# Moving a routing exponential from the first to the second half of a tile's routing

## The chip, the cores and the metric

The kernel runs on one core of a Trainium2 chip. The metric is the device time of one execution in microseconds. Five engines share the work, each with its own queue that it takes in order: PE (TensorE, matmuls), DVE (VectorE), ACT (ScalarE), POOL (GpSimd) and SP (SyncE, which here only issues transfers).

## The reference, cut to what matters

Three layers follow each other. Block attention over 8 heads gives a token matrix x of 4608 rows and 512 columns. A dense layer maps it through 2048 hidden columns. A routed layer then sends each token to one of 8 experts:

```
out = softmax(q_c @ k_c.T / 8) @ v_c              # 64-row chunks
x   = relu(x @ w_in)**2 @ w_out                   # 512 -> 2048 -> 512
logits = x @ w_gate + modality_bias[modality_id]
e_idx  = argmax(logits);  probs = exp(logits - max)
gate   = probs[e_idx] / (sum(probs) + 1e-9)       # probs[e_idx] is exp(0) = 1
out[mask] = gate * (relu(x[mask] @ w1[e]) @ w2[e])
```

The changed instruction computes `exp(logits - max)` of one tile of 128 tokens, and with it the sum over the 8 experts. Only that sum is used: the gate is one over it.

## The kernel before, in words

The 4608 tokens are 36 tiles of 128. Nine blocks of four tiles pass through the dense layer one after the other. For a block, `mm1` runs 16 steps of 12 matmuls (x times w_in, in three 16-bit passes), and `mm2` runs 16 steps of 12 matmuls (hidden times w_out, four steps a tile). After the nine blocks comes the expert stage: `slot_mm1` and `slot_mm2` take 128 gathered rows of one expert at a time.

One mm1 step fills one PSUM tile `hp`, of which there are two. ACT must empty it with a Relu (`r<-hp`) before the step after the next can start. From `r`, ACT makes a 16-bit square (`big<-r`), DVE a 32-bit square (`g<-r`), and POOL their difference. Five tiles `r` exist.

Attention of later tiles, the splitting of the expert weights (`piece_split`: ACT writes `wss`, DVE its low half, SP stores it; one buffer) and the routing of finished tiles run beside this on ACT, DVE, POOL and SP, with a few small matmuls on PE.

Routing of tile i begins when its last mm2 step is done: `x2_evac` (ACT and DVE take the result out of PSUM into `xs`), `x2_tr` (SP transposes it), then two halves. `route_a` has 12 small matmuls into `lp`, seven DVE instructions (`lg`, the maximum, its index in two instructions, `ef`, `oh`, `nm`) and, before the change, the Exp on ACT (`ex<-lg,nm`, which also sums into `se`). `route_b` has two small matmuls into `rp`, DVE's `dj`, `di`, `run`, `ga`, its reciprocal and `mt`, and a POOL scatter of `mt` to DRAM (`meta`). `ga` is the first reader of `se`.

The order on every engine's queue is made once, when the program is written. Work beside the matmuls stands in a list with due times. Between two steps, `flush` issues what is due. An event whose engine is over its budget (`COST` gives each event a cost on ACT and on DVE, `back` sums it up) is put off, at most by 30 units of planned time; `route_a`, `route_b` and one small norm share a PSUM tile, and are kept two steps apart from each other. Then `evac` issues the Relu and what follows it for the step that was issued before, and then the next step's matmuls are issued. So the first event issued in a `flush` stands ahead of the Relu of the previous step on ACT's queue.

Of the kernel before, what the change touches and what calls it, by code (L numbers as in the profile page):

```python
# [8 lines left out]
F32 = mybir.dt.float32  # L9
# [4 lines left out]
AF = mybir.ActivationFunctionType  # L14
ALU = mybir.AluOpType
# [14 lines left out]
def kernel(  # L30
# [17 lines left out]
    E, _, F2 = w1.shape  # L48
# [18 lines left out]
    sm_p = ctx.enter_context(tc.tile_pool(name="sm", bufs=4))  # L67
# [17 lines left out]
    def act(out, in_, func=AF.Copy, **kw):  # L85
        nc.scalar.activation(out=out, in_=in_, func=func, **kw)  # L86

    def stt(out, in0, s, in1, op0, op1, **kw):
        nc.vector.scalar_tensor_tensor(out=out, in0=in0, scalar=s, in1=in1, op0=op0, op1=op1, **kw)  # L89

    def ts2(out, in0, s1, s2, op0, op1=None, eng=None):
        if op1 is None:
            (eng or nc.vector).tensor_scalar(out=out, in0=in0, scalar1=s1, scalar2=None, op0=op0)  # L93
        else:
            (eng or nc.vector).tensor_scalar(out=out, in0=in0, scalar1=s1, scalar2=s2, op0=op0, op1=op1)  # L95
# [486 lines left out]
    def route_a(i):  # L582
        a = x2[i]
        lp = ps_r.tile([128, 512], F32, tag="r", name="lp")
        n = 0
        for la, lb in PASSES:
            for kk in range(KD):
                nc.tensor.matmul(lp[:, 0:E], lhsT=a["xt"][:, la * KD + kk, :], rhs=wgs[:, lb, kk, :],
                                 start=n == 0, stop=n == 3 * KD - 1)
                n += 1  # L590
        lg = sm_p.tile([128, E], F32, tag="lg", name="lg")
        stt(lg, lp[:, 0:E], a["ui"][:, 0:1], bias_t[:, i, :], ALU.mult, ALU.add)
        m8 = sm_p.tile([128, 8], F32, tag="m8", name="m8")
        i8 = sm_p.tile([128, 8], U32, tag="i8", name="i8")
        nc.vector.max(out=m8, in_=lg)
        nc.vector.max_index(out=i8, in_max=m8, in_values=lg)
        ef = sm_p.tile([128, 1], F32, tag="ef", name="ef")
        nc.vector.tensor_copy(out=ef, in_=i8[:, 0:1])
        oh = sm_p.tile([128, E], F16, tag="oh", name="oh")
        ts2(oh, iota8, ef[:, 0:1], None, ALU.is_equal)  # L600
        nm = sm_p.tile([128, 1], F32, tag="nm", name="nm")
        ts2(nm, m8[:, 0:1], -1.0, None, ALU.mult)
        ex = sm_p.tile([128, E], F32, tag="ex", name="ex")
        se = sm_p.tile([128, 1], F32, tag="se", name="se")
        act(ex, lg, AF.Exp, bias=nm[:, 0:1], accum_out=se)
        a["oh"], a["se"] = oh, se

    def route_b(i):
        a = x2[i]
        rp = ps_r.tile([128, 512], F32, tag="r", name="rp")  # L610
        nc.tensor.matmul(rp[:, 0:E], lhsT=ones_h, rhs=run, start=True, stop=False)
        nc.tensor.matmul(rp[:, 0:E], lhsT=tri_h, rhs=a["oh"], start=False, stop=True)
        dj = sm_p.tile([128, E], F32, tag="dj", name="dj")
        df = sm_p.tile([128, 1], F32, tag="df", name="df")
        di = sm_p.tile([128, 1], I32, tag="di", name="di")
        stt(dj, rp[:, 0:E], 1.0, a["oh"], ALU.mult, ALU.mult, accum_out=df)
        nc.vector.tensor_copy(out=di, in_=df)
        nc.vector.tensor_tensor(out=run, in0=run, in1=a["oh"], op=ALU.add)
        mt = sm_p.tile([128, 2], F32, tag="mt", name="mt")
        nc.gpsimd.tensor_copy(out=mt[:, 0:1], in_=tok[:, i:i + 1])  # L620
        ga = sm_p.tile([128, 1], F32, tag="ga", name="ga")
        ts2(ga, a["se"], 1e-9, None, ALU.add)
        nc.vector.reciprocal(out=ga, in_=ga)
        ts2(mt[:, 1:2], ga, a["ui"][:, 0:1], SWG / (SW1 * SW2), ALU.mult, ALU.mult)
        nc.gpsimd.indirect_dma_start(  # L625
            out=meta[:, :], out_offset=bass.IndirectOffsetOnAxis(ap=di[:, 0:1].bitcast(U32), axis=0),
            in_=mt, in_offset=None,
        )
        x2.pop(i)
# [42 lines left out]
    def map_a1():  # L672
        assert (route_b, SEEN - 1) in done and (route_b, SEEN) not in done
        ci = counts(0.0, "a")
        tf = sm_p.tile([128, E], F32, tag="tf", name="tf")
        m8 = sm_p.tile([128, 8], F32, tag="m8", name="m8a")
        i8 = sm_p.tile([128, 8], U32, tag="i8", name="i8a")
        ea = const.tile([128, 1], F32, name="ea")
        on = const.tile([128, E], F32, name="on")
        rw = sm_p.tile([128, 1], F32, tag="rw", name="rwa")  # L680
        nc.vector.tensor_copy(out=tf, in_=ci)
        nc.vector.max(out=m8, in_=tf)
        nc.vector.max_index(out=i8, in_max=m8, in_values=tf)
        nc.vector.tensor_copy(out=ea, in_=i8[:, 0:1])
        ts2(rw, ea, float(TPE), None, ALU.mult)
        mp["mga"] = meta_gather(rw, EARLY, "a")
        ts2(on, iota8, ea[:, 0:1], None, ALU.is_equal)
        rg = const.tile([1, 1], I32, name="rga")
        nc.vector.tensor_copy(out=rg, in_=i8[0:1, 0:1])
        mp.update(ea=ea, on=on, rga=rg)  # L690
# [139 lines left out]
    def once(fn, s):  # L830
# [14 lines left out]
    COST = {  # L845
        attn_split: (0.95, 1.14), attn_vsplit: (1.04, 1.2), attn_max: (0.0, 1.2), attn_exp: (0.52, 0.0),
        attn_p: (0.0, 1.5), attn_psplit: (0.52, 0.0), attn_x: (0.48, 0.6), x_sq: (0.52, 0.0),
        x_norm: (0.0, 0.2), piece_split: (0.95, 1.14), x2_evac: (1.2, 1.1), route_a: (0.3, 0.9),
        route_b: (0.0, 0.8),
    }  # L850

    def uses_r(fn, a):
        return fn in (route_a, route_b) or fn is x_norm and where[a[0]][3] == 3
# [11 lines left out]
    def at_chain(chain):  # L865
# [3 lines left out]
        attn_split: ((attn_s, 2),), attn_s: ((attn_max, 1),), attn_max: ((attn_psplit, 2),),  # L869
        attn_psplit: ((attn_ptr, 2),), attn_vsplit: ((attn_pv, 2),), attn_ptr: ((attn_pv, 2),), attn_pt: ((attn_pv, 2),), attn_pv: ((attn_x, 1),),  # L870
        x_norm: tuple((x_sq, d) for d in range(4)), x2_evac: ((x2_tr, 4),), x2_tr: ((route_a, 2),), piece_split: ((piece_store, 1),),
        piece_load: ((piece_split, 4),),
    }
# [193 lines left out]
    for su, (b0, nt, sb) in enumerate(supers):  # L1067
        for j in sb:
            n = subs[j][1]
            ta = T  # L1070
            for c in range(KF * n // 4):
                steps.append((T, mm1, (j, c)))
                T += STEP
            span.append((ta, T))
        for t, qq in M2 if su == 0 else [(t, qq) for t in range(nt) for qq in range(4)]:
            steps.append((T, mm2, (su, t, qq)))
            T += STEP
            if qq < 3:
                continue
            i = b0 + t  # L1080
            d = (2.0, 7.0, 9.7) if i >= NTILE - 2 else (4.0, 11.0, 16.0)
            ch = [(T, x2_evac, (i,)), (T + d[0], x2_tr, (i,)), (T + d[1], route_a, (i,)), (T + d[2], route_b, (i,))]
            if i == SEEN - 1:
                ch += [(T + 20.0, map_a1, ()), (T + 30.0, map_a2, ()), (T + 35.0, once, (slot_gather, 0)),
                       (T + 35.1, once, (slot_gather, 1)), (T + 35.2, once, (slot_gather, 2)),
                       (T + 35.3, once, (slot_gather, 3)), (T + 45.0, once, (slot_tr, 0)),
                       (T + 50.0, once, (slot_tr, 1)), (T + 55.0, once, (slot_tr, 2)), (T + 60.0, once, (slot_tr, 3))]
            if i == NTILE - 1:
                ch += [(T + 12.4, map_b1, ()), (T + 18.4, map_b2, ()), (T + 18.5, once, (slot_w1, EARLY)),
                       (T + 18.6, once, (slot_w2, EARLY)), (T + 26.0, map_b3, ()),  # L1090
                       (T + 26.1, once, (slot_gather, EARLY)), (T + 26.2, once, (slot_gather, EARLY + 1)),
                       (T + 30.0, once, (slot_tr, EARLY)), (T + 32.0, once, (slot_tr, EARLY + 1))]
            at_chain(ch)
        if su == len(supers) - 1:
            for x, h, t in ((0, 0, 0.1 - STEP * 4 * nt), (0, 1, 0.2 - STEP * 4 * nt), (1, 0, 2.1), (1, 1, 20.0)):
                at_time(T + t, early_w, x, h)
# [154 lines left out]
```

## Time and profile before

| what | us |
|---|---|
| median of 3 runs | 1309.19 |
| lowest and highest | 1309.03, 1309.44 |
| the profiled execution's own time | 1314.08 |
| its span, first to last instruction | 1312.3 |

The profile describes one execution, which took 4.89 us longer than the median of the three runs. A timeline row gives the start of a group of equal instructions, its length and, in brackets, how long its engine sat idle before and what ended that. Ends of matmuls are modelled: the mean matmul of 512 columns lasts 380 ns, while in a group of 12 they start closer than that. The dense stage with attention and routing fills the span up to about 872 us, the expert stage the rest.

### The profile page before, as it was taken

The page shows a single profiled execution, that of the slowest core. Times are in us where ns is not written, and L with a number is a line of the kernel's source. Part 1 is how long each engine was busy: PE and PEld are TensorE (multiplying, and loading weights), DVE is VectorE, ACT ScalarE, POOL GpSimd, SP SyncE. Part 2 cuts the span into 40 slices and gives each one's busy share as a digit, 9 for nine tenths or more (in the row PEclk, how much of TensorE's full clock was granted, in tenths as well). Part 3 has the DMA queues.
Part 4 walks back from the last instruction along what each step waited for, and adds up shares of the span by engine and source line. Part 5 has one row for each costly group of instructions (what it writes and reads, how often), then busy time and mean ns, then how long its engine had stood idle before and what let it go on. Part 6 is the DMA issues. An engine that isn't in the chain of part 4 may idle for free.

```text
span 1312.3 us, 28854 instructions
## 1 busy us (share of the span) xinstructions
PE 1234.1 (94%) x11836; PEld 700.0 (53%) x11836; DVE 673.7 (51%) x1467; ACT 553.7 (42%) x978; POOL 407.3 (31%) x386
## 2 busy tenths in 40 slices
PE   5898999999999999999999999998999993999994
PEld 4444444445444444444444444466777772777773
DVE  6899785785876877867857836132111110111110
ACT  5887564563654654745645635211111110111110
POOL 4488351440431522422604604312122110111111
PEclk9899999999999999999999999999999996999998
DMA  9355536756477558477566451644223358322221
GB/s 376 140 186 147 113 113 190 197 170 200 133 222 174 159 154 227 124 201 179 167 195 162 139 135 33 201 83 157 69 77 82 79 168 186 74 73 74 74 73 41
DMA packets 172346, 188.54 MB, mean 144 GB/s; under 512 B 119547, under 2 KB 119587, under 8 KB 171186
## 3 DMA queue, kind: packets, MB, share of 16 engines
q1 hardware_dynamic: 128930, 157.72, 42.0%
q0 software_dynamic: 7376, 20.01, 4.8%
q10 hardware_dynamic: 35904, 8.92, 4.3%
q8 instruction: 94, 1.54, 0.5%
q14 instruction: 42, 0.34, 0.1%
HBM read 240.23 MB, written 53.08 MB: 224 GB/s over the span
## 4 chain that ended last, share of the span: by engine, by line
PE 43%; issue 22%; DMA 15%; DVE 12%; ACT 6%; POOL 0%; SPq 0%; POOLq 0%; DVEq 0%; ACTq 0%
PE op L558 23%; PE hp L543 14%; DMA out_dram<-o,tib 10%; DVE g L89 2%; DMA wsp<-wss 2%; PE xp L433 1%; DVE wss L89 1%; PE hp L805 1%; DMA big<-in_w_in_dram 1%; DVE qkt L89 1%; ACT r L86 1%; ACT wss L86 1%; ACT big L86 1%; DVE wl L89 1%; PE op L819 1%
## 5 line engine op out<-in xcount | busy, mean ns | idle before, releaser
L543 PE MATMUL hp<-xt,big 128*128 128x512 f16 x1728 | 387.7, 380 | 9.6 <-ACT r L86 9.4
L558 PE MATMUL op<-big,big 128*128 128x512 f16 x1728 | 384.5, 380 | 0.5 <-POOL big L523 0.5
L543 PEld LDWEIGHTS <-big 128*128 128x128 f16 x1728 | 164.1, 98 | 200.6 <-issue 14.7
L558 PEld LDWEIGHTS <-big 128*128 128x128 f16 x1728 | 165.1, 98 | 194.3 <-issue 2.8
L523 POOL TENSOR_TENSOR big<-g,big 128x512 f16<-128x512 f32 x144 | 177.1, 1234 | 209.3 <-DVE g L89 140.8
L89 DVE SCALAR_TENSOR_TENSOR ht<-hp,ht 128x512 f16<-128x512 f32 x74 | 51.2, 692 | 355.4 <-ACT ht L86 355.4
L805 PE MATMUL hp<-xgt,big 128*128 128x128 f16 x3552 | 210.0, 222 | 24.9 <-DMA xgt<-xg 24.9
L805 PEld LDWEIGHTS <-big 128*128 128x128 f16 x3552 | 206.3, 99 | 33.7 <-issue 25.6
L819 PE MATMUL op<-big,ht 128*128 128x512 f16 x888 | 197.6, 379 | 0.0
L89 DVE SCALAR_TENSOR_TENSOR g<-r,bq 128x512 f32<-128x512 f32 x138 | 136.9, 996 | 31.7 <-ACT r L86 30.6
L819 PEld LDWEIGHTS <-ht 128*128 128x128 f16 x888 | 85.4, 98 | 96.2
L825 POOL DMA_INDIRECT out_dram<-o,tib x33 | 33.5, 1014 | 291.4 <-ACT o L86 281.9
L89 DVE SCALAR_TENSOR_TENSOR wss<-wst,wss 128x1024 f16<-128x1024 f32 x64 | 91.5, 1430 | 60.5 <-ACT wss L86 59.9
L86 ACT ACTIVATE ht<-hp 128x512 f16<-128x512 f32 x74 | 44.2, 597 | 177.5 <-PE hp L805 177.4
L625 POOL DMA_INDIRECT meta<-mt,di x36 | 40.9, 1137 | 213.2 <-issue 81.1
L86 ACT ACTIVATE big<-r,bls 128x512 f16<-128x512 f32 x138 | 99.5, 722 | 6.5 <-DVE bli L95 0.7
L86 ACT ACTIVATE r<-hp 128x512 f32<-128x512 f32 x138 | 80.9, 587 | 48.2 <-PE hp L543 30.8
L86 ACT ACTIVATE wss<-wst 128x1024 f16<-128x1024 f32 x64 | 67.0, 1047 | 56.4 <-DMA wsp<-wss 37.5
L86 ACT ACTIVATE o<-op,fsb 128x512 f32<-128x512 f32 x33 | 22.7, 687 | 152.7 <-PE op L819 152.7
L406 POOL TENSOR_TENSOR ps<-ee,ps 128x512 f16<-128x512 f32 x32 | 44.2, 1381 | 89.8 <-ACT ps L86 88.4
L86 ACT ACTIVATE ex<-lg,nm 128x8 f32<-128x8 f32 x36 | 10.8, 301 | 116.4 <-DVE nm L93 116.4
L89 DVE SCALAR_TENSOR_TENSOR qkt<-qk,qkt 128x1024 f16<-128x1024 f32 x32 | 44.3, 1384 | 12.5 <-ACT qkt L86 11.7
(174 smaller groups left out, 984.2 us busy)
## 6 DMA issues: line engine op xcount, KB each, us to landing
big<-wsp SPq DMA_DIRECT2D x72, 2048.0 KB
wst<-in_w_dram SPq DMA_DIRECT2D x64, 512.0 KB
wsp<-wss SPq DMA_DIRECT2D x64, 512.0 KB
qk<-in_qk_dram SPq DMA_DIRECT2D x36, 512.0 KB
vv<-in_v_dram SPq DMA_DIRECT2D x36, 256.0 KB
x2d<-xs SPq DMA_DIRECT2D x36, 256.0 KB
big<-in_w_in_dram SPq DMA_DIRECT2D x16, 512.0 KB
wl<-in_w_out_dram SPq DMA_DIRECT2D x16, 512.0 KB
```

Of the source, the lines that this page charges most:

```text
L86: nc.scalar.activation(out=out, in_=in_, func=func, **kw)
L89: nc.vector.scalar_tensor_tensor(out=out, in0=in0, scalar=s, in1=in1, op0=op0, op1=op1, **kw)
L406: nc.gpsimd.tensor_tensor(out=a["ps"][:, 1], in0=pf, in1=a["ps"][:, 0], op=ALU.subtract)
L433: nc.tensor.matmul(xp[h, hp, 64 * c:64 * c + 64], lhsT=vs[h, la, c, hp, :], rhs=pt[h, lb * KD + hp, 64 * c:64 * c + 64], start=n == 0, sto ...
L523: nc.gpsimd.tensor_tensor(out=lo, in0=q32.rearrange("p (f n) -> p f n", f=nf), in1=hi, op=ALU.subtract)
L543: nc.tensor.matmul(hp[:, q_ * n:(q_ + 1) * n], lhsT=wi[:, la, kk, f * 128:f * 128 + 128], rhs=x[:, lb, kk, :], start=i == 0, stop=i == 3 * ...
L558: nc.tensor.matmul(ps, lhsT=g[:, la, f, t * 128:t * 128 + 128], rhs=wo[:, lb, f, :], start=f == 0 and n == 0, stop=f == KF - 1 and n == 2)
L625: nc.gpsimd.indirect_dma_start(out=meta[:, :], out_offset=bass.IndirectOffsetOnAxis(ap=di[:, 0:1].bitcast(U32), axis=0), in_=mt, in_offset ...
L805: nc.tensor.matmul(hp[:, f4 * 128:f4 * 128 + 128], lhsT=w[:, la, kk, f * 128:f * 128 + 128], rhs=xt[:, lb * KD + kk, :], start=n == 0, sto ...
L819: nc.tensor.matmul(ps, lhsT=ht[:, la, f, :], rhs=w[:, lb, f, :], start=f == 0 and n == 0, stop=f == KF2 - 1 and n == 2)
L825: nc.gpsimd.indirect_dma_start(out=out[:, :], out_offset=bass.IndirectOffsetOnAxis(ap=slot[s][0].bitcast(U32), axis=0), in_=o, in_offset=N ...
```

## The change

The three lines that allocate `ex` and `se` and issue the Exp leave `route_a` and stand in `route_b`, behind the update of `run`. `lg` and `nm` are kept for it. In the table `COST`, the 0.3 of ACT time moves from `route_a` to `route_b` too.

```diff
         nm = sm_p.tile([128, 1], F32, tag="nm", name="nm")
         ts2(nm, m8[:, 0:1], -1.0, None, ALU.mult)
-        ex = sm_p.tile([128, E], F32, tag="ex", name="ex")
-        se = sm_p.tile([128, 1], F32, tag="se", name="se")
-        act(ex, lg, AF.Exp, bias=nm[:, 0:1], accum_out=se)
-        a["oh"], a["se"] = oh, se
+        a["oh"], a["nm"], a["lg"] = oh, nm, lg
 
     def route_b(i):
...
         nc.vector.tensor_tensor(out=run, in0=run, in1=a["oh"], op=ALU.add)
+        ex = sm_p.tile([128, E], F32, tag="ex", name="ex")
+        se = sm_p.tile([128, 1], F32, tag="se", name="se")
+        act(ex, a["lg"], AF.Exp, bias=a["nm"][:, 0:1], accum_out=se)
         mt = sm_p.tile([128, 2], F32, tag="mt", name="mt")
         nc.gpsimd.tensor_copy(out=mt[:, 0:1], in_=tok[:, i:i + 1])
         ga = sm_p.tile([128, 1], F32, tag="ga", name="ga")
-        ts2(ga, a["se"], 1e-9, None, ALU.add)
+        ts2(ga, se, 1e-9, None, ALU.add)
...
-        x_norm: (0.0, 0.2), piece_split: (0.95, 1.14), x2_evac: (1.2, 1.1), route_a: (0.3, 0.9),
-        route_b: (0.0, 0.8),
+        x_norm: (0.0, 0.2), piece_split: (0.95, 1.14), x2_evac: (1.2, 1.1), route_a: (0.0, 0.9),
+        route_b: (0.3, 0.8),
```

Every engine issues the same instructions as before, in the same number; only their order differs. Up to planned step 39 of 288 the events fall into the same steps. From step 40 to step 249 attention, routing and weight pieces move by at most three steps either way, and from step 250 on each event is in its old step again.

On ACT, in the mm1 steps of the fourth block, where tile 14 is routed, before (r is the Relu's result, hp its PSUM tile; the numbers only tell buffers apart):

```order
L86 ACTIVATE r_6097<-hp 128x512
L86 ACTIVATE big_98<-r_6097,bls 128x512
L86 ACTIVATE ex,se<-lg,nm 128x8
L86 ACTIVATE r_6147<-hp 128x512
L86 ACTIVATE big_98<-r_6147,bls 128x512
L86 ACTIVATE xt<-xp 128x4x128
L86 ACTIVATE wss<-wst 128x1024
```

The same place on ACT now:

```order
L86 ACTIVATE r_6097<-hp 128x512
L86 ACTIVATE big_98<-r_6097,bls 128x512
L86 ACTIVATE r_6144<-hp 128x512
L86 ACTIVATE big_98<-r_6144,bls 128x512
L86 ACTIVATE xt<-xp 128x4x128
L86 ACTIVATE ps<-ee 128x512
L86 ACTIVATE wss<-wst 128x1024
```

The Relu that stood behind the Exp follows the square of the step before it directly; `ps`, which belongs to attention, comes a little earlier.

On ACT, six steps later, where the second half of tile 14's routing now stands:

```order
L86 ACTIVATE wss<-wst 128x1024
L86 ACTIVATE r_6318<-hp 128x512
L86 ACTIVATE big_98<-r_6318,bls 128x512
L86 ACTIVATE ex,se<-lg,nm 128x8
L86 ACTIVATE r_6358<-hp 128x512
L86 ACTIVATE big_98<-r_6358,bls 128x512
```

Here the Exp again stands ahead of a Relu, but its inputs `lg` and `nm` were made six steps earlier. Of the 36 Exps, 17 stood directly ahead of a Relu `r<-hp` before, and 23 do now.

On DVE, the second half of tile 14's routing now:

```order
L89 SCALAR_TENSOR_TENSOR wss<-wst,wss 128x1024
L89 SCALAR_TENSOR_TENSOR g_6320<-r_6318,bq 128x512
L89 SCALAR_TENSOR_TENSOR dj,df<-rp,oh 128x8
L614 CAST di<-df 128x1
L615 TENSOR_TENSOR run<-run,oh 128x8
L93 TENSOR_SCALAR ga<-se 128x1
L623 RECIPROCAL ga<-ga 128x1
L95 TENSOR_SCALAR mt<-ga,ui 128x1
L89 SCALAR_TENSOR_TENSOR g_6360<-r_6358,bq 128x512
```

DVE's instructions of this half and their order are the same as before; `ga` now reads a sum that ACT makes in the same half.

At the end of the routing, on ACT, from the Exps of tiles 33 and 34 to that of tile 35, the last (`xs` is taken out for tile 35; `ht` belongs to the expert stage), before:

```order
L86 ACTIVATE ex,se<-lg,nm 128x8 x2
L86 ACTIVATE xs,ss<-op 128x512
L86 ACTIVATE xs<-op,tss 128x512
L86 ACTIVATE ht<-hp_11967 128x512
L86 ACTIVATE ht<-hp_12047 128x512
L86 ACTIVATE ht<-hp_11967 128x512
L86 ACTIVATE ex,se<-lg,nm 128x8
L86 ACTIVATE ht<-hp_12047 128x512
```

The same place on ACT now, from tile 33's Exp on:

```order
L86 ACTIVATE ex,se<-lg,nm 128x8
L86 ACTIVATE xs,ss<-op 128x512
L86 ACTIVATE xs<-op,tss 128x512
L86 ACTIVATE ht<-hp_11964 128x512
L86 ACTIVATE ex,se<-lg,nm 128x8
L86 ACTIVATE ht<-hp_12047 128x512
L86 ACTIVATE ht<-hp_11964 128x512
L86 ACTIVATE ht<-hp_12047 128x512
L86 ACTIVATE ex,se<-lg,nm 128x8
```

Tile 34's Exp moved behind the last tile's `xs` and the first `ht`, and the last tile's Exp behind one more `ht`.

## Rows read from the trace of the kernel before

**Rows 1.** The page: span, PE's busy time, granted clock in 40 slices.
```profile
span 1312.3 us, 28854 instructions
...
PE 1234.1 (94%) x11836; PEld 700.0 (53%) x11836; DVE 673.7 (51%) x1467; ACT 553.7 (42%) x978; POOL 407.3 (31%) x386
...
PEclk9899999999999999999999999999999996999998
```

**Rows 2.** PE's waits: what waited, for what, total us, times, longest.
```profile
PE hp L805 <- DMA xgt<-xg: 24.9, 2, 21.2
PE hp L543 <- ACT r L86: 9.4, 10, 1.9
...
PE lp L588 <- DVE dj L89: 0.9, 1, 0.9
...
PE rp L612 <- DVE nm L93: 0.4, 1, 0.4
```

**Rows 3.** Timeline of PE at the longest of these: start, length, instruction, idle before.
```profile
428.25 0.45 PE L588 MATMUL lp<-wgs,x2t 128*128 128x8 f16 x12
428.55 2.75 PE L543 MATMUL hp<-xt,big 128*128 128x512 f16 x12
433.18 2.75 PE L543 MATMUL hp<-xt,big 128*128 128x512 f16 x12 [1.87 <-ACT r L86]
```

**Rows 4.** Timeline of ACT at the same place.
```profile
426.49 0.72 ACT L86 ACTIVATE big<-r,bls 128x512 f16<-128x512 f32 x1
432.25 0.30 ACT L86 ACTIVATE ex<-lg,nm 128x8 f32<-128x8 f32 x1 [5.04 <-DVE nm L93]
...
432.55 0.57 ACT L86 ACTIVATE r<-hp 128x512 f32<-128x512 f32 x1
...
433.79 0.57 ACT L86 ACTIVATE xt<-xp 128x512 f16<-128x512 f32 x1
```

**Rows 5.** Timeline of DVE at the same place.
```profile
430.73 0.22 DVE L89 SCALAR_TENSOR_TENSOR lg<-lp,ui,bias_t 128x8 f32<-128x8 f32 x1
...
432.08 0.14 DVE L93 TENSOR_SCALAR nm<-m 128x1 f32<-128x1 f32 x1
433.23 0.75 DVE L89 SCALAR_TENSOR_TENSOR g<-r,bq 128x512 f32<-128x512 f32 x1 [1.01 <-ACT r L86]
```

**Rows 6.** Timeline of PE: first of the ten waits for r, and the odd one.
```profile
155.43 0.81 PE L543 MATMUL hp<-xt,big 128*128 128x512 f16 x3 [1.36 <-ACT r L86]
...
552.58 1.67 PE L543 MATMUL hp<-xt,big 128*128 128x512 f16 x7 [0.36 <-ACT r L86]
```

**Rows 7.** Timeline of ACT ahead of the odd one.
```profile
550.98 1.06 ACT L86 ACTIVATE wss<-wst 128x1024 f16<-128x1024 f32 x1 [4.04 <-DMA wsp<-wss]
```

**Rows 8.** Groups of PE instructions by line: busy us, mean ns, idle before.
```profile
L543 PE MATMUL hp<-xt,big 128*128 128x512 f16 x1728 | 387.7, 380 | 9.6 <-ACT r L86 9.4
```

**Rows 9.** ACT's waits: total us, times, longest.
```profile
ACT ex L86 <- DVE nm L93: 116.4, 36, 7.7
...
ACT ee L86 <- DVE ee L365: 37.6, 16, 5.2
ACT wss L86 <- DMA wsp<-wss: 37.5, 15, 7.6
...
ACT ps L86 <- DVE ee L384: 30.2, 16, 4.1
```

**Rows 10.** DVE's waits, and its oh: ns min, median, max.
```profile
DVE dj L89 <- PE rp L612: 16.1, 12, 4.1
...
L93 DVE TENSOR_SCALAR oh<-iota,ef x36: 231/231/1681, 149.4 to 882.5; 128x8 f16<-128x8 f32 x36
```

**Rows 11.** Timelines of ACT and DVE at the last tile's routing.
```profile
883.34 0.60 ACT L86 ACTIVATE ht<-hp 128x512 f16<-128x512 f32 x1
...
884.58 0.15 DVE L89 SCALAR_TENSOR_TENSOR dj<-rp,oh 128x8 f32<-128x8 f32 x1
...
884.92 0.15 DVE L93 TENSOR_SCALAR ga<-se 128x1 f32<-128x1 f32 x1
```

## The prediction

> **What bounds the kernel now.** I read the page first. PE is busy for 1234.1 of 1312.3 us, so time can only come from the 78 us in which it is not, or from work taken off it, and the change takes none off [rows 1]. Next I read PE's waits, to see which of those 78 us a routing instruction could own. The largest entry, 24.9 us for gathered rows, lies in the expert stage, whose order the change leaves alone. The next one is 9.4 us in ten waits: an mm1 matmul waits for ACT's Relu to empty its PSUM tile [rows 2].
>
> Then I took the longest of the ten on three engines. On PE, tile 14's `lp` runs at 428.25, one mm1 step follows, and the step after it waits 1.87 us until 433.18 [rows 3]. On ACT, the Relu that this step needs stands behind an Exp, and the Exp sits idle for 5.04 us for `nm` [rows 4]. On DVE, `lg` starts only at 430.73, 2.48 us after `lp`, because DVE is busy with earlier work; `nm` starts at 432.08, the Exp at 432.25. DVE then idles 1.01 us for that same Relu [rows 5]. So DVE is late, but it is not DVE that PE waits for: the Relu's own input had been in PSUM since about 428.5, and only the place of the Exp in ACT's queue held it back. What ends last is the chain `lp`, DVE's seven instructions, Exp, Relu.
>
> I checked the other nine the same way. Eight, from the one at 155.43 on, show the same Exp ahead of the Relu. The odd one is 0.36 us at 552.58, where ACT had waited for the store of a weight piece [rows 6, 7]. All nine stand where a tile is routed beside mm1; beside mm2 the same idling of ACT costs PE nothing. That is why the Exp's 116.4 us of idle time on ACT [rows 9] shrink to 9.0 us on PE.
>
> **What the change removes.** The Exp now stands in the second half, at least two steps behind the first, with `lg` and `nm` long made. The nine waits lose their cause: 9.4 − 0.4 = 9.0 us [rows 2, 6].
>
> A wait in that table is counted from the modelled end of the matmul before it. A group of 12 takes 2.75 us and its last matmul 0.38, so the array starts one every (2.75 − 0.38) / 11 = 0.215 us, but each is shown for 0.38 [rows 3, 8]. Each wait therefore costs 0.38 − 0.215 = 0.165 us more than it shows: nine make 1.5 us. Together 10.5 us.
>
> [...] By the waits alone the sum would be 9.0, by the starts 10.5; the trace's groups of 12 side with the starts.
>
> [...]
>
> **What the change adds.** No instruction is added; the Exp's own 0.30 us [rows 4] is paid in both orders.
>
> `ga` on DVE must now wait for an Exp issued a moment before. Behind it in DVE's queue stand the next `g` and parts of attention. In 23 of 36 places the Exp stands directly ahead of the Relu of the step just finished, so ACT gets to it before `dj`, which needs a matmul behind that step; I cost these at nothing. In the other 13 it may stand behind Relu and square, which take 433.79 − 432.55 = 1.24 us [rows 4], and itself takes 0.30 before what follows, 1.54 in all; `dj` to `ga` covers 0.34 of it [rows 11]. That bounds the wait at 1.2 us a place if DVE is free. DVE met `dj` free, waiting for PE, in 12 of 36 places [rows 10]; in the other 24 it came late, and the Exp will be there. As PE waits on DVE for 1.3 us in routing in this whole trace [rows 2], I take zero, and keep 12 × 1.2 = 14.4 us as the bad end.
>
> `lg` and `nm` live longer, in four buffers each. At most two tiles stand between their halves, so no new wait: zero.
>
> At the end, the last tile's Exp moves behind one more `ht`. That `ht` starts at 883.34 and takes 0.60, the Exp 0.30, so it ends at about 884.3; `ga` of that tile runs at 884.92 [rows 11]. The chain into the expert stage is not longer: zero. If that cover were gone, it would be some tenths of a microsecond, once.
>
> The moved events between steps 40 and 249 are the unknown. ACT also waits for attention's `ee` and `ps` and for `wss`: 37.6 + 37.5 + 30.2 = 105.3 us in 47 waits [rows 9], of which one reached PE, for 0.36. A shift of up to three steps can carry others in front of a Relu, or away from one. The low end is below zero: the 0.36, and the `lp` and `rp` waits of 0.9 and 0.4 [rows 2], with 0.165 for each, are 2.2 us that may also vanish. The high end is that nine of the 47 take over, at the mean of the nine: 9.0 / 9 + 0.165 = 1.17 us each, 10.5 us. I take 1.5 us: one of the mean size and one like the odd one, as only one of 47 reached PE so far.
>
> **The sum**, against the profiled execution: 1314.08 − 10.5 + 1.5 = 1305.1 us. It stands 4.89 above the median of the runs, so the median should be 1300.2 us.
>
> **The rivals.** A: other waits of ACT take over. With the Exp gone, ACT comes sooner to an `ee`, `ps` or `wss` that is not ready, and the Relu behind it is late again. For it: DVE is late at these places [rows 5], and there are 47 such waits [rows 9]. Against it: in the order before they reached PE once, and at tile 14 nothing but the Relu follows the square now. Taking back four to six waits of 1.17 gives 1303 to 1306; seven or more, 1306.6 up to about 1309. The full case would look like no change.
>
> B: slower, because DVE waits at `ga`. If in the 12 places where DVE was free it stands for 1.2 us, and all of it reaches PE through `lp`, `rp` or attention, that is 14.4 us: 1309.2 − 10.5 + 14.4 = 1313.1. It decides above 13.1 us (10.5 and 2.6), 1.1 us for each of the 12. Against it: DVE's being late by more than 2 us, as at `lg` [rows 3, 5], reached PE there only through ACT.
>
> [...]
>
> C: the gain is larger, with the 2.2 us of the other waits gone and nothing given back: 1309.2 − 12.7 = 1296.5.
>
> **How the numbers follow.** What a measurement of this kernel can tell from no change is about 0.2%, 2.6 us. The forecast, 1297 to 1304.5, gets 0.70. A in part, 1304.5 to 1306.6, gets 0.10 and is still faster. A in full gets 0.12. C below 1297 gets 0.03, B 0.05. So faster 0.83, same 0.12, slower 0.05. The range 1297 to 1307 holds the forecast and A in part, about 0.81; the likeliest case alone is 1297 to 1304.5.
>
> **What would show it.** In the profile after, ACT's wait of `ex` for `nm`, 116.4 us in 36, is gone. PE's wait for `r` falls from 9.4 to under 3 us, and what is left of it stands behind `wss`, `ee` or `ps`. At tile 14, the mm1 steps follow `lp` without a wait. DVE gets a new line, `ga` waiting for `ex`, of under 20 us in all, and PE's waits on DVE stay near 1.3 us. The 24.9 us of the expert stage stay. I am wrong if the wait for `r` is as long as before under other names (A), if `ga`'s wait is followed by waits of PE on `oh`, `dj` or `xt` (B), or if the wait is gone and the time is not.

## The result and the profile after

The changed kernel takes 1295.53 us (median of 4 runs, 1294.8 to 1299.36) and the kernel before, run beside it, 1309.32 us (4 runs, 1309.03 to 1310.62). The ratio is 0.9896, with a 95% interval of 0.9871 to 0.9920: faster by 13.8 us, where the prediction had 9.0 us. The time lies 1.5 us below its range.

The profiled execution took 1299.36 us, 14.72 us less than that of before. The page of the changed kernel, against [rows 1]: span, busy time, granted clock in 40 slices.

```profile
span 1297.6 us, 28861 instructions
...
PE 1230.9 (95%) x11836; PEld 699.8 (54%) x11836; DVE 677.1 (52%) x1467; ACT 558.4 (43%) x978; POOL 410.7 (32%) x386
...
PEclk9999999999999999999999999998999996999997
```

The engines are about as busy as before, and the mean granted clock is 0.98 in both. What went is mostly idle time of PE, 78.2 us of the span before and 66.7 now. Of the four entries of PE's waits shown in [rows 2], one is left, the gathered rows of the expert stage:

```profile
PE hp L805 <- DMA xgt<-xg: 24.5, 2, 20.8
```

The same view over 130 to 860 us has no entry at all. Before, the same stretch held the 9.4 us for `r`, 0.9 for `lp` and 0.4 for `rp`. At tile 14, PE, against [rows 3] (start, length, instruction):

```profile
423.05 0.45 PE L588 MATMUL lp<-wgs,x2t 128*128 128x8 f16 x12
423.35 7.93 PE L543 MATMUL hp<-xt,big 128*128 128x512 f16 x36
```

Three mm1 steps, 36 matmuls, follow `lp` in one unbroken group. ACT at the same place, against [rows 4]:

```profile
423.25 0.60 ACT L86 ACTIVATE r<-hp 128x512 f32<-128x512 f32 x1 [1.24 <-PE hp L543]
423.88 0.72 ACT L86 ACTIVATE big<-r,bls 128x512 f16<-128x512 f32 x1
424.50 0.58 ACT L86 ACTIVATE xt<-xp 128x512 f16<-128x512 f32 x1
```

DVE there, against [rows 5]:

```profile
425.53 0.22 DVE L89 SCALAR_TENSOR_TENSOR lg<-lp,ui,bias_t 128x8 f32<-128x8 f32 x1
...
426.88 0.14 DVE L93 TENSOR_SCALAR nm<-m 128x1 f32<-128x1 f32 x1
426.94 0.73 DVE L89 SCALAR_TENSOR_TENSOR g<-r,bq 128x512 f32<-128x512 f32 x1
```

DVE starts `lg` 2.48 us after `lp`, exactly as late as before. Nobody pays for it now: `g` follows `nm` at once. ACT's waits, against [rows 9] (total us, times, longest):

```profile
ACT r L86 <- PE hp L543: 77.4, 85, 5.2
...
ACT ee L86 <- DVE ee L365: 49.6, 20, 6.4
ACT wss L86 <- DMA wsp<-wss: 38.8, 16, 7.2
ACT ps L86 <- DVE ee L384: 37.9, 16, 3.2
...
ACT ex L86 <- DVE nm L93: 8.6, 6, 2.3
```

ACT still idles for long, but for other reasons. The Exp's wait for `nm` is down from 116.4 us in 36 places to 8.6 in six, so it is nearly, not wholly, gone. The Relu now waits for PE's matmuls, 77.4 us, where it waited 30.8 before:

```profile
ACT r L86 <- PE hp L543: 30.8, 37, 3.6
```

In such a wait PE is the engine that is waited for, so PE loses nothing by it: its own list of waits over 130 to 860 us is empty. The waits for `ee`, `wss` and `ps` grew from 105.3 to 126.3 us, and none of them reached PE.

Where the time went is read from the starts of the same matmul in both traces. I take the stretch from the first matmul of mm1 step 20, the last before the orders part, to the first expert matmul. Below it is called the dense stretch.

| stretch | before | after | difference |
|---|---|---|---|
| start to mm1 step 20 | 151.31 | 150.76 | -0.55 |
| dense stretch | 720.76 | 707.67 | -13.09 |
| expert stage to the span's end | 440.22 | 439.21 | -1.01 |

The two outer stretches hold the same instructions, in the same order but for the last Exps among the first `ht`, and the runs below show how they vary by chance. In the dense stretch the difference grows by jumps. Nine of them, at the nine waits, are 1.53, 1.01, 1.22, 0.83, 2.04, 0.98, 0.69, 0.56 and 1.62, together 10.48 us. The remaining 2.6 us lie at 552 us (about 0.5), at 680 to 687 us (about 1.6), and in pieces too small to place.

### The profile page after: what moved, and what is told of

Read it like the earlier page. It is cut to its first block, busy times and chain, and to the rows that moved or that the text cites. A ratio compares the mean times of both kernels' runs of the same rounds, so it can differ in the third digit from the quotient of the medians.

```text
span 1297.6 us, 28861 instructions
## 1 busy us (share of the span) xinstructions
PE 1230.9 (95%) x11836; PEld 699.8 (54%) x11836; DVE 677.1 (52%) x1467; ACT 558.4 (43%) x978; POOL 410.7 (32%) x386
## 5 line engine op out<-in xcount | busy, mean ns | idle before, releaser
L523 POOL TENSOR_TENSOR big<-g,big 128x512 f16<-128x512 f32 x144 | 184.3, 1282 | 215.7 <-DVE g L89 147.0
L805 PE MATMUL hp<-xgt,big 128*128 128x128 f16 x3552 | 209.3, 221 | 24.5 <-DMA xgt<-xg 24.5
L89 DVE SCALAR_TENSOR_TENSOR g<-r,bq 128x512 f32<-128x512 f32 x138 | 145.2, 1056 | 20.5 <-ACT r L86 19.3
L86 ACT ACTIVATE r<-hp 128x512 f32<-128x512 f32 x138 | 82.0, 594 | 102.7 <-PE hp L543 77.4
L406 POOL TENSOR_TENSOR ps<-ee,ps 128x512 f16<-128x512 f32 x32 | 46.9, 1467 | 134.9 <-issue 97.1
L625 POOL DMA_INDIRECT meta<-mt,di x36 | 38.1, 1057 | 144.2 <-issue 86.8
L89 DVE SCALAR_TENSOR_TENSOR qkt<-qk,qkt 128x1024 f16<-128x1024 f32 x32 | 48.0, 1500 | 7.4 <-ACT qkt L86 6.1
L86 ACT ACTIVATE xs<-op 128x512 bf16<-128x512 f32 x36 | 21.2, 589 | 63.5 <-PE op L558 57.2
```

Of the source, the lines that this page charges most:

```text
L406: nc.gpsimd.tensor_tensor(out=a["ps"][:, 1], in0=pf, in1=a["ps"][:, 0], op=ALU.subtract)
L523: nc.gpsimd.tensor_tensor(out=lo, in0=q32.rearrange("p (f n) -> p f n", f=nf), in1=hi, op=ALU.subtract)
L625: nc.gpsimd.indirect_dma_start(out=meta[:, :], out_offset=bass.IndirectOffsetOnAxis(ap=di[:, 0:1].bitcast(U32), axis=0), in_=mt, in_offset ...
L805: nc.tensor.matmul(hp[:, f4 * 128:f4 * 128 + 128], lhsT=w[:, la, kk, f * 128:f * 128 + 128], rhs=xt[:, lb * KD + kk, :], start=n == 0, sto ...
```

## Experiments

The dense stretch of each profiled run, in us, is given beside the ratio of medians. Each ratio is against the kernel before, measured beside that run, since medians taken at different times differ: those of the kernel before are 1309.32, 1310.75, 1311.54 and 1311.05 us. Three programs were run twice: the changed kernel (again as e5), e1 (again as e6) and e3 (again as e7). Each program has one trace for each time it was run, and the kernel before has one. For e5 I had expected 707 to 709 us in the dense stretch and 1290 to 1300 in all; it took 707.7 and 1294.66.

| run | what differs | ratio, 95% interval | dense stretch |
|---|---|---|---|
| before | | 1 | 720.8 |
| changed | | 0.9896 (0.9871 to 0.9920) | 707.7 |
| e5 | changed, again | 0.9878 (0.9843 to 0.9913) | 707.7 |
| e1 | Exp moved, old order of the rest | 0.9925 (0.9887 to 0.9963) | 714.8 |
| e6 | as e1, again | 0.9905 (0.9868 to 0.9943) | 709.9 |
| e2 | new order, Exp in the first half | 1.0027 (0.9997 to 1.0057) | 720.0 |
| e3 | Exp in the first half, Relu ahead of it | 0.9889 (0.9840 to 0.9939) | 709.1 |
| e7 | as e3, again | 0.9889 (0.9855 to 0.9923) | 709.7 |
| e4 | changed, Exp behind the Relu | 0.9896 (0.9846 to 0.9945) | 708.5 |
| e9 | changed, Relu first in every flush | 0.9904 (0.9870 to 0.9937) | 709.6 |
| e10 | as e4, ga made to wait longer | 0.9962 (0.9926 to 0.9998) | 713.0 |

**e1 and e6: the Exp alone.** The changed kernel with the old table, so that only the Exp's place on ACT differs from before.

```diff
-        x_norm: (0.0, 0.2), piece_split: (0.95, 1.14), x2_evac: (1.2, 1.1), route_a: (0.0, 0.9),
-        route_b: (0.3, 0.8),
+        x_norm: (0.0, 0.2), piece_split: (0.95, 1.14), x2_evac: (1.2, 1.1), route_a: (0.3, 0.9),
+        route_b: (0.0, 0.8),
```

> The Exp alone moves to the second half; the cost table stays, so every other instruction keeps its old place on every engine. Theory Q (the Exp's place in ACT's queue): the nine waits of PE for the Relu go, 10.5 us; the waits of lp and rp at 680 to 686 (0.9 and 0.4) and the 0.36 behind the weight piece stay, since nothing there is moved: about 1298.5 to 1299.5, some 3 us above the changed kernel. Rival O (the shifted order does it): little, 1305 or more.

> The Exp alone moved, once more. In its first profile one wait of 3.6 us at a weight piece, and slow matmuls behind it, took 5.8 us of the gain. Theory S (the store that the piece waits for varies from run to run): the wait is between 0 and 4 us again and not the same as before, and everything else as in the first profile: 151 us to the first expert matmul in 708 to 715. Rival: the order without the cost table always has this wait at 3 us or more, so the moved cost earns about 6 us: 714 or more.

Measured: the nine jumps are there, 10.54 us in all, and so are the two at 680 to 687 us, 0.5 and 1.07. The waits at `rp` and `lp`, which I had expected to stay, are thus gone too; whether the Exp removed them is taken up below. The median of e1, 1303.02 us, lies between the two expectations. In its trace a longer wait took 6.0 us back, 3.3 in the wait and 2.7 in slower matmuls behind it; PE and ACT there:

```profile
548.15 8.03 PE L543 MATMUL hp<-xt,big 128*128 128x512 f16 x24 [3.64 <-ACT r L86]
...
546.55 1.06 ACT L86 ACTIVATE wss<-wst 128x1024 f16<-128x1024 f32 x1 [7.33 <-DMA wsp<-wss]
```

A Relu stands behind the split of a weight piece, which waits for the store of the piece before it. This is the odd wait of before [rows 6, 7], ten times as long. In e6, the same program, it is the same place with a shorter store:

```profile
546.74 5.34 PE L543 MATMUL hp<-xt,big 128*128 128x512 f16 x24 [1.63 <-ACT r L86]
...
545.15 1.06 ACT L86 ACTIVATE wss<-wst 128x1024 f16<-128x1024 f32 x1 [5.32 <-DMA wsp<-wss]
```

So in the old order this wait depends on how long one store takes. From the end of DVE's half of a piece to the start of the split that waits for its store, it is 7.6 us before, 8.3 in e6 and 10.3 in e1, and PE's wait is 0.36, 1.63 and 3.64 us; the rest of the growth, 0.5 us, is that PE comes to this place earlier after that half. In e3 and e7 below, which have the old order too, it is 7.0 and 7.4 us, and PE does not wait here. In the order of the changed kernel the wait occurred in neither of its two profiles.

**e2: the order alone.** The kernel before with the new table; the Exp stays in `route_a`.

```diff
-        x_norm: (0.0, 0.2), piece_split: (0.95, 1.14), x2_evac: (1.2, 1.1), route_a: (0.3, 0.9),
-        route_b: (0.0, 0.8),
+        x_norm: (0.0, 0.2), piece_split: (0.95, 1.14), x2_evac: (1.2, 1.1), route_a: (0.0, 0.9),
+        route_b: (0.3, 0.8),
```

> Only the cost table changes: the order of all other work is that of the changed kernel, the Exp stays in the first half. Theory Q: the Exp still stands ahead of the Relu and waits for nm, so PE's wait for r stays at 8 to 11 us in about nine places, and only the 2 to 3 us of the shifted order are gained: 1305 to 1308. Rival O: most of the 13.8 us are gained, 1297 or less.

Measured: no gain that can be told, where I had expected 2 to 3 us. PE's wait for `r` and ACT's for `nm` are about as they were:

```profile
PE hp L543 <- ACT r L86: 10.6, 10, 2.4
...
ACT ex L86 <- DVE nm L93: 123.2, 36, 7.7
```

From 130 to 866 us the first of these lines is PE's only one: the odd wait and those at `lp` and `rp` are missing although the Exp is still in the first half, and the waits behind the Exp come out longer than the 9.0 us of before. By themselves the moved events neither cost the 1.5 us of the prediction nor bring the gain. With the Exp moved, the new order has 707.7 where the old has 709.9 and 714.8, and most of that difference is the odd wait.

**e3 and e7: the Exp stays, the Relu goes ahead of it.** If the Exp harms only by standing ahead of the Relu, `evac` (which issues that Relu) in front of it must do what the change does.

```diff
         se = sm_p.tile([128, 1], F32, tag="se", name="se")
+        evac()
         act(ex, lg, AF.Exp, bias=nm[:, 0:1], accum_out=se)
```

> As the kernel before, but where an Exp of the first half stood directly ahead of a Relu and its square, these two are issued ahead of it (15 places, ACT alone is reordered). The Exp still waits for nm as long as it did. Theory Q: what cost time was the Relu behind the Exp, so the nine waits go as they do with the Exp moved: 1298 to 1300, and ACT's wait of ex for nm stays long (60 us or more). Rival: the idling of ACT itself costs, whatever stands behind: 1305 or more.

> The Relu issued ahead of the Exp of the first half, once more, beside the changed kernel on the same chip. Theory: its lead over the changed kernel in the first batch came from a shorter wait in the expert stage (10.9 against 24.5 us), which is chance: from 151 us to the first expert matmul 708 to 711 again, and the whole time within 0.4% of the changed kernel. Rival: it is faster by 4 us or more, with the expert stage shorter again.

Measured: the same gain, with the Exp still in the first half and still idle for 80 us. PE's wait for `r` and ACT's for `nm` in e3:

```profile
PE hp L543 <- ACT r L86: 0.7, 1, 0.7
...
ACT ex L86 <- DVE nm L93: 81.5, 35, 7.7
```

ACT's idling is not the cost; what stood behind it was. The 0.7 us left is one place where the Exp's wait delays the Relu of the next step instead; e7 has it too, and 0.4 us behind a weight piece. That e3's median was 3.4 us below the changed kernel's, and below what I had expected, is not shown to be a lead of the edit: the ratios are the same, and in its profile the expert stage's wait for gathered rows is short.

```profile
PE hp L806 <- DMA xgt<-xg: 10.9, 2, 7.2
```

In e7, the same program, it is 19.2, and e7 and e5, measured side by side, cannot be told apart.

**e4: a later Exp, so that `ga` waits.** The changed kernel with Relu and square of the finished step issued ahead of the Exp in `route_b`; its other parts follow behind `mt`. The new helper `evac_act`, whose body is left out here, issues parts 0 and 2 of `mm1_part`, the Relu and the square.

```diff
         se = sm_p.tile([128, 1], F32, tag="se", name="se")
+        late = evac_act()
         act(ex, a["lg"], AF.Exp, bias=a["nm"][:, 0:1], accum_out=se)
...
+        for n in late:
+            mm1_part(n, 1)
+            mm1_part(n, 3)
         nc.gpsimd.indirect_dma_start(
```

> As the changed kernel, but in the second half the Relu and the square of the step just finished are issued ahead of the Exp, so that ga on DVE has to wait for them too (22 Exps move on ACT). Theory: DVE's wait at ga, about 1.2 us in 18 places where DVE is free, reaches no matmul: 1295 to 1297, within 1 us of the changed kernel. Rival B: DVE's wait reaches PE through dj, lp or attention: 1300 or more.

Measured: DVE has a line that the changed kernel has not.

```profile
DVE ga L93 <- ACT ex L86: 13.4, 17, 1.2
```

The longest is 1.2 us, the bound that the prediction worked out, and the waits fall in 17 places. The dense stretch is 0.85 us longer than the changed kernel's, and the ratio of medians is the same; the median, 1297.99 us, is between the two expectations. The 0.85 us have one place: PE waits 0.8 us at `tp`, near the end of the dense stretch, for `mgc`, which gathers the finished routing for the expert stage. The last `ga` ahead of it comes 1.90 us after its `rp`, and 0.59 in the changed kernel, where PE does not wait at `tp`.

**e10: the same, with a price high enough to see.** Six more Exps of the same tile, whose results nobody reads, ahead of the real one.

```diff
+        for _ in range(6):
+            pe_ = sm_p.tile([128, E], F32, tag="ex", name="ex")
+            ps_ = sm_p.tile([128, 1], F32, tag="se", name="se")
+            act(pe_, a["lg"], AF.Exp, bias=a["nm"][:, 0:1], accum_out=ps_)
         act(ex, a["lg"], AF.Exp, bias=a["nm"][:, 0:1], accum_out=se)
```

> The order of the run in which Relu and square stand ahead of the Exp in the second half, with six more Exps of the same tile (their results are not used) ahead of the one that ga reads. Each is a 0.29 us Exp and its sum, so ACT reaches the real Exp about 2 to 3 us later at all 36 places. Theory (DVE has room between the mm1 steps, and only what stands ahead of a Relu on ACT reaches PE): DVE's wait of ga for the Exp grows from 13.4 us in 17 to over 60 us in 30 or more, the longest 3 to 4 us; PE's waits between 130 and 872 us stay under 3 us in all; from step 20 of mm1 to the first expert matmul 708 to 712 us; median 1295 to 1302. Rival (a late ga costs what it waits, through g, lp, rp or attention behind it on DVE's queue): new waits of PE on DVE or ACT of over 10 us in all, that stretch 718 us or more, median 1307 or more. In between, 712 to 718, some of the places have room and others not, and PE's waits name those that have none.

Measured: between the two expectations in the dense stretch, 713.0 us. DVE's wait at `ga` grew less than I had expected (over 60 us in 30 places). It, and all of PE's waits from 150 to 866 us:

```profile
DVE ga L93 <- ACT ex L86: 43.7, 24, 2.9
```

```profile
PE tp L682 <- DVE mgc L679: 2.8, 1, 2.8
PE hp L552 <- ACT r L86: 0.7, 2, 0.5
PE np L480 <- DVE lg L89: 0.7, 1, 0.7
```

Another 30.3 us of waiting on DVE went with 4.5 us more in the dense stretch than in e4, but not spread over the places. The largest wait is at `tp` again: the last `ga` ahead of it now comes 3.88 us after its `rp`. Of the 0.7 us at `r`, 0.5 stand behind the Exps themselves on ACT and 0.2 behind a late `ps`; the 0.7 at `np` stand behind a `lg` that DVE runs only after a late weight piece, with no wait at `ga` near. Before 650 us PE waits for nothing, though five of DVE's waits at `ga` there are of 2.7 to 2.9 us. So `tp` is the one place where a late `ga` is shown to reach PE. The median is 1304.43 us, above what the theory gave; how much of that is a late `ga` and how much the six Exps on ACT these runs do not show.

**e9: the Relu first, always.** The changed kernel with `evac` at the start of every `flush`, so that nothing stands ahead of a finished step's Relu.

```diff
         kept = []
+        evac()
```

> The changed kernel, with the Relu, squares and difference of the step just finished issued ahead of everything else that is due at that step, so that no other wait of ACT can stand in front of a Relu issued late. Theory: in the changed kernel no Relu is late any more, so nothing is left to gain in the dense stage: 707 to 709 us from 151 us to the first expert matmul, same time within 0.3%; a gain only in runs where a weight piece's store is slow. Rival: DVE's and POOL's share of the step, now ahead of routing and attention, delays lp, rp or xp: 711 or more.

Measured: no gain over the changed kernel, whose Relu waits were already none. The dense stretch, 709.6 us, lies between the two expectations, and the median, 1300.15 us, is 0.4% above e5's beside it where I had expected 0.3% at most. There is one new wait, from the same view over 130 to 865 us:

```profile
PE tp L665 <- DVE mgc L662: 1.8, 1, 1.8
```

That is the place of e4 and e10: here the square on DVE stands ahead of the routing, and the last `ga` comes 1.90 us after its `rp` without waiting for an Exp. No kernel tried beats the changed one by more than the intervals.

## Why the prediction was wrong

**The nine waits (right).** They vanished, and the nine jumps are 10.48 us where the sum had 10.5. By the waits alone it would have been 9.0. That a wait costs 0.165 us more than it shows is borne out. e3 shows the cause as the prediction gave it: the place of the Exp in ACT's queue, not its idling and not DVE's lateness.

**The granted clock.** The sum has no term for it, and none was needed: over the dense stretch it is 1.00 in both profiles.

**`ga` (right).** It has no entry in DVE's waits of the changed kernel; the new line of under 20 us that I expected is not there. The line of `dj`, against [rows 10], shows that DVE comes to it early more often than before, and still finds the Exp done:

```profile
DVE dj L89 <- PE rp L609: 25.6, 18, 4.1
```

The bad end, 12 x 1.2 = 14.4 us with all of it reaching PE, was far too dear: in e4 seventeen waits of up to 1.2 us cost under a microsecond. Nor did `ga` itself take longer. The durations of `ga`, of its reciprocal and of `mt` in the changed kernel (ns, min, median, max), and those of `run` just ahead of them:

```profile
L93 DVE TENSOR_SCALAR ga<-se x36: 141/146/150, 156.5 to 871.3; 128x1 f32<-128x1 f32 x36
L623 DVE RECIPROCAL ga<-ga x36: 163/164/166, 156.7 to 871.5; 128x1 f32<-128x1 f32 x36
L95 DVE TENSOR_SCALAR mt<-ga,ui x36: 213/214/216, 156.9 to 871.7; 128x1 f32<-128x1 f32 x36
```

```profile
L615 DVE TENSOR_TENSOR run<-run,oh x36: 150/153/1105, 156.5 to 871.2; 128x8 f16<-128x8 f16 x36
```

Each of the three at `ga` varies by at most 9 ns. `run` took up to 1105 ns against a median of 153, and up to 1148 in the kernel before; the eight of the changed kernel that took over 600 ns each lie beside a `big<-g,big` of POOL. `oh` took up to 1291 ns against a median of 231, and up to 1681 before [rows 10]. What made these two longer no run tested.

**The end of the routing (right)** as far as it can be told: the difference is 13.1 us after the last jump and 13.09 at the first expert matmul.

**The moved events (the step that failed).** The prediction took 1.5 us to be given back, "one of the mean size and one like the odd one, as only one of 47 reached PE so far". Measured is the other sign: 13.09 - 10.48 = 2.6 us more came off. That is rival C, to which I gave 0.03; the low end that I had worked out for this term, -2.2 us, was near, and I gave it no weight. This step makes 4.1 us of the 5.7 us by which the profiled pair beat the sum; the other 1.56 are the two outer stretches, chance of the run. By the medians the miss is 4.7 us (1300.2 against 1295.53). The size of 2.6 us comes from one pair of traces and is in part luck: some 1.5 of it (0.5 each at 552 us, at `rp` and at `lp`) is missing in e3 and e7 too, which have the old order and the Exp in the first half, and goes back to slower stores in the one trace of the kernel before. Two parts were wrong.

First, the wait of `lp` was put down to the moved events, as something that might vanish, and the Exp's idling beside mm2 was said to cost PE nothing. At `lp`, which stands among mm2's matmuls, the Exp had a second path to PE. Before, on ACT, DVE and PE in turn:

```profile
680.43 0.30 ACT L86 ACTIVATE ex<-lg,nm 128x8 f32<-128x8 f32 x1 [2.01 <-DVE nm L93]
...
680.73 1.04 ACT L86 ACTIVATE qkt<-qk 128x1024 f16<-128x1024 f32 x1
```

```profile
680.25 0.15 DVE L93 TENSOR_SCALAR nm<-m 128x1 f32<-128x1 f32 x1
681.81 1.23 DVE L89 SCALAR_TENSOR_TENSOR qkt<-qk,qkt 128x1024 f16<-128x1024 f32 x1 [1.41 <-ACT qkt L86]
...
686.45 0.16 DVE L89 SCALAR_TENSOR_TENSOR dj<-rp,oh 128x8 f32<-128x8 f32 x1
```

```profile
686.67 0.44 PE L588 MATMUL lp<-wgs,x2t 128*128 128x8 f16 x12 [0.91 <-DVE dj L89]
```

ACT makes attention's `qkt` only after the Exp. DVE starts `nm` at 680.25 and then idles 1.41 us for that `qkt`, and everything behind it, `dj` included, is that much later; PE waits 0.91. In e1, whose DVE order is that of before:

```profile
675.52 1.05 ACT L86 ACTIVATE qkt<-qk 128x1024 f16<-128x1024 f32 x1
...
677.89 0.30 ACT L86 ACTIVATE ex<-lg,nm 128x8 f32<-128x8 f32 x1
```

```profile
677.45 0.15 DVE L93 TENSOR_SCALAR nm<-m 128x1 f32<-128x1 f32 x1
677.51 1.22 DVE L89 SCALAR_TENSOR_TENSOR qkt<-qk,qkt 128x1024 f16<-128x1024 f32 x1
...
682.15 0.16 DVE L89 SCALAR_TENSOR_TENSOR dj<-rp,oh 128x8 f32<-128x8 f32 x1
```

`qkt` is ahead, DVE runs on, and `lp` has no wait. From `nm` to `dj` it is 6.20 us before and 4.70 here, so the Exp's place is worth 1.5 us on DVE. In e3 and e7 the Exp keeps its old place here, DVE idles the same 1.41 us, and `lp` waits 0.34 and 0.43 us. That path is shown, at that size.

The rest of `lp`'s 0.91 us, and the 0.35 at `rp`, are not the Exp's. They go back to the store of a weight piece, by which DVE came to `oh` about 1 us later: 6.68 us after the earlier `lp` before, 5.61 in e1. Before, on ACT and PE:

```profile
672.37 1.06 ACT L86 ACTIVATE wss<-wst 128x1024 f16<-128x1024 f32 x1 [7.62 <-DMA wsp<-wss]
...
673.43 0.44 PE L588 MATMUL lp<-wgs,x2t 128*128 128x8 f16 x12
...
680.40 0.17 PE L612 MATMUL rp<-oh,tri_h 128*128 128x8 f16 x1 [0.35 <-DVE nm L93]
```

In e3, with the Exp in the same place:

```profile
664.44 1.06 ACT L86 ACTIVATE wss<-wst 128x1024 f16<-128x1024 f32 x1 [6.73 <-DMA wsp<-wss]
...
666.56 0.44 PE L588 MATMUL lp<-wgs,x2t 128*128 128x8 f16 x12
...
673.03 0.17 PE L613 MATMUL rp<-oh,tri_h 128*128 128x8 f16 x1
...
678.73 0.44 PE L588 MATMUL lp<-wgs,x2t 128*128 128x8 f16 x12 [0.34 <-DVE dj L89]
```

The split `wss` starts 1.06 us ahead of the earlier `lp` before, and 2.0 to 2.2 us ahead of it in e1, e3, e6 and e7; of these five traces only that of before has a wait at `rp`. I had followed every wait for `r` back to its cause, and for the waits of `lp` and `rp` read only the first name, DVE.

Second, the waits for `ee`, `wss` and `ps` were priced by their number, one in 47. They are not alike. What reaches PE is decided by what stands behind a wait in the queue, and the one that counted was `wss` ahead of a Relu, above all at one place of the old order (e1, e6). In the new order the pieces fall elsewhere, and no wait of ACT reached PE in the changed kernel's two profiles. Where each piece stands could have been read from the order before the run; how long its store takes could not.

**The rivals.** A is refuted by the empty list from 130 to 860 us. In the old order it would have been partly right: e1 gave back 6.0 us by just that mechanism. B is refuted by e4 at its own size; e4 and e10, with three times its waiting at `ga`, show the one place, `tp`, where it begins. C happened.

What stays open is why the stores of weight pieces and the expert stage's wait differ between runs of one program (below), and the 0.5 us in pieces too small to place. In the changed kernel the Exp's new place and the moved order each suffice against the wait at `lp` (e1, e2), so its share there cannot be told. The odd wait was not tried with a second buffer for `wss`.

## What to carry to other kernels

On an engine that takes its queue in order, the price of a waiting instruction is what stands behind it (in e3 the Exp still waited for 81.5 us, and PE for `r` only 0.7): look for the instruction that empties the bottleneck's buffer, and move either of the two. When such a wait goes, follow every other wait of the bottleneck back through all its engines before calling it someone else's; a small one may be the same cause by a second path, and its neighbour may be another cause altogether. A wait for a transfer ahead of such an instruction is a risk that changes from run to run (PE waited 0.36, 1.63 and 3.64 us before, in e6 and in e1), and one profile shows only one draw of it.

## What the runs showed of the hardware

One wait of PE cost more than itself. After the 3.64 us in e1, the granted clock of the stretches from 548 us on was 0.50, then 0.80 (stretch, length, PE's busy time, clock, DMA share, GB/s), and 24 matmuls took 8.03 us, where those behind the 1.63 us in e6 took 5.34:

```profile
548.00:552.00 4.00, 3.85 (x10) 0.50 0.36 135
552.00:556.00 4.00, 4.00 (x16) 0.80 0.13 26
```

So 8.03 - 5.34 = 2.7 us came on top of the wait. After the 2.42 us in e2 the clock was 1.00 over the next 5.6 us.

The expert stage's wait for gathered rows lay between 10.9 and 24.9 us in these profiles, with two values for each program that ran twice: 24.5 and 19.5 (changed, e5), 19.0 and 24.9 (e1, e6), 10.9 and 19.2 (e3, e7). The expert stage lasted 428.5 us at 10.9 and 440.1 us at 24.9. A difference of some microseconds between single runs of this kernel can come from there alone.
